# First attention of a two-block network: one v tile ahead of the step loop, projection groups a step earlier, row transposes issued later

The kernel runs on one core of one Trainium2 chip. The metric is the device time of one execution in microseconds. Where a ratio is given, it is the mean time of one kernel's runs over the mean of the kernel before's runs in the same rounds, so it is not quite the ratio of the medians quoted beside it.

## The reference

```python
# x: 2048 rows of 576, four residual layers A, B, A, B on normed rows
def _A_ref(x, wqkv, wo):              # 32 heads of 18, window of 8 positions, every second one
    qkv = (x @ wqkv)...               # q, k, v
    logits = einsum(q, gathered k) * 18 ** -0.5; masked where the position is negative
    return softmax(logits) @ gathered v @ wo
def _B_ref(x, w_in, w_sp, b_sp, w_out):
    z = gelu(x @ w_in)                # 4608 wide, two halves z1, z2
    g = w_sp @ layernorm(z2) + b_sp   # 2048 x 2048 over the rows
    return (z1 * g) @ w_out
x = x + _A_ref(layernorm(x), ...); x = x + _B_ref(layernorm(x), ...)   # twice
```

The change concerns the first A layer alone.

## The kernel before

Attention runs in 38 steps, two for each tile of 112 query rows (16 heads each). A step computes the next step's logits, exponentiates them on ScalarE, multiplies this step's probabilities with v (`PV`), and then runs whatever the table `at(step, ...)` lists for it: projection groups (`PG`) for the second half of the sequence, v tiles (`VW`), the output projection (`WO`), and the normed rows for the next layer (`LN_XN` on POOL, then `LN_T`, a transposing DMA into `xnT`).

```python
def PG(d, qk, cc, dve, queues=(nc.sync, nc.gpsimd)):
    ...                                   # 5 matmuls 128x512, cast into a staging slot
    for dst, src in moves:                # one copy a head: staging slot -> QK
        self.dma(dst, src, eng=queues[dma_rr[0] % len(queues)])
...
if hf == 1:                               # in PV, after the second half of a tile
    if t < NT - 2:
        nc.sync.dma_start_transpose(out=oT[...], in_=o_t[:nq, :])
...
# the table
for k_, (d, qk, cc) in enumerate(pgs):
    at(2 + k_ if li == 0 else (k_ * PG_END) // len(pgs), PG, d, qk, cc, True)
for t in range(nvw, NT):
    for hh in range(2):
        if li == 0 and t == nvw:
            at(hh, VW, t, hh, True)
        else:
            at(2 * t - 2 + hh, VW, t, hh, 2 * t - 2 + hh >= PG_END and hh == 0)
for i in range(NS):
    ...
    at(s - 5, XO, i);  at(s, WO, i, 0);  at(s + 1, WO, i, 1)
    at(s + 1, LN_STATS, i);  at(s + 2, LN_XN, i);  at(s + 2, XST, i)
    if i < NS - 1:
        at(s + 4, LN_T, i)
...
for k_, (d, qk, cc) in enumerate(pre):    # six projection groups ahead of the loop
    if k_ == (2 if li == 0 else 0):
        L_mm(0); EXP(0)
    PG(d, qk, cc, li > 0 or k_ < 4, q2)
for s in range(NST):
    if s + 1 < NST:
        L_mm(s + 1); EXP(s + 1)
    PV(s)
    for f, a in table.pop(s, []):
        f(*a)
```

In the text, "the copies" are the `QK` moves of `PG`, "o transposes" are those in `PV`, and "row transposes" are `LN_T`. All DMA transposes, about half of the copies, and the row loads and stores go through the SyncE queue; the o transposes of the last two tiles are made by TensorE. A block d of the projection is up to 128 columns of q and of k; d=4 is the last. "Late waits" are waits for o transposes near the end of the loop. A cold step or spell is one at half clock. In the profile lines, `L_ps` are the logits, `O_ps` the product of probabilities and v, `pv` a v tile, `pp` a projection group, `pw` the output projection, and `pz` the first product of layer B.

The softmax here doesn't subtract the row's maximum and nothing guards it: scores larger than these inputs give would overflow.

## Time and profile before

| | before |
|---|---|
| median of three runs | 1196.94 us (1193.07 to 1198.15) |
| span of the profiled run | 1193.7 us |
| TensorE busy | 1182.4 us |
| granted clock, mean | 0.996 |

TensorE is the bound; idle gaps and lowered clock are all that an order of instructions can change. The prediction shows the lines for both: two holes of TensorE in the first attention (hole 1 near 46 us, hole 2 near 90 us), each with a spell at half clock behind it.

### The profile page before, as it was taken

What the parts mean: (1) busy time and instruction counts of PE and PEld (TensorE: products, weight loads), DVE (VectorE), ACT (ScalarE), POOL (GpSimd) and SP (SyncE); (2) the same over time, 40 slices, a digit from 0 to 9 for tenths busy, and PEclk for the clock granted to TensorE, in tenths of its full rate; (3) what the DMA queues carried; (4) which work ended last, traced back from release to release, by engine and by line L of the source; (5) the groups of instructions that cost most, each with busy time, mean ns of one, the idle gap of its engine ahead of it and who ended that gap; (6) DMA issues with size and microseconds to landing.
All of it is one profiled execution on the core that took longest, in us unless ns stands there. A gap on an engine that the chain in (4) does not pass through costs nothing.

```text
span 1193.7 us, 20761 instructions
## 1 busy us (share of the span) xinstructions
PE 1182.4 (99%) x8554; PEld 621.8 (52%) x8554; DVE 548.0 (46%) x1207; ACT 376.0 (31%) x592; POOL 275.3 (23%) x383
## 2 busy tenths in 40 slices
PE   9999999999999999999999999999999999999998
PEld 5566644444444444457755775444444444444677
DVE  9687677333233233244455776763223223223311
ACT  6477677211111111201156786770110110111000
POOL 4677773100000000001144777530000000000000
PEclk9899999999999999999999999999999999999999
DMA  8989892000000000049646899900000000000332
GB/s 198 190 160 220 166 221 67 23 1 12 12 12 12 12 1 12 2 139 297 169 97 111 190 236 186 224 11 12 12 12 1 12 12 12 12 1 25 127 105 73
DMA packets 178103, 101.21 MB, mean 85 GB/s; under 512 B 134335, under 2 KB 159359, under 8 KB 178008
## 3 DMA queue, kind: packets, MB, share of 16 engines
q1 hardware_dynamic: 165144, 78.13, 30.9%
q0 software_dynamic: 6512, 16.00, 5.2%
q10 hardware_dynamic: 6352, 5.75, 1.6%
q8 instruction: 67, 1.10, 0.4%
q14 instruction: 28, 0.23, 0.1%
HBM read 42.39 MB, written 16.53 MB: 49 GB/s over the span
## 4 chain that ended last, share of the span: by engine, by line
PE 94%; DMA 2%; SPq 1%; POOL 1%; DVE 1%; issue 0%; ACT 0%; DVEq 0%; POOLq 0%
PE pg L879 42%; PE pz L861 12%; PE po L933 12%; PE pz L783 11%; PE pp L401 4%; PE pw L493 3%; PE pv L378 3%; PE O_ps L456 3%; PE L_ps L436 2%; PE pzs L783 1%; SPq L77 1%; DMA QK<-win2a 1%; POOL QK L77 1%; DMA oT<-o_t 1%; DMA oT<-in_A_x_dram 1%
## 5 line engine op out<-in xcount | busy, mean ns | idle before, releaser
L879 PE MATMUL pg<-Wq,Z 128*128 128x512 bf16 x2304 | 502.8, 379 | 0.0
L879 PEld LDWEIGHTS <-Z 128*128 128x128 bf16 x2304 | 225.5, 98 | 271.7
L883 DVE TENSOR_TENSOR g_tmp<-pg,ln_xn 128x512 f32<-128x512 f32 x144 | 99.5, 691 | 428.9 <-PE pg L879 428.9
L873 ACT ACTIVATE z1T<-pz 128x1024 bf16<-128x1024 f32 x72 | 73.7, 1023 | 513.9 <-PE pz L861 513.7
L77 POOL DMA_DIRECT2D wout<-in_B_w_out_dram x4 | 4.2, 1062 | 604.6 <-PE pg L879 604.6
L445 ACT ACTIVATE P_sb<-L_ps 128x896 bf16<-128x896 f32 (+1 forms) x152 | 126.9, 888 | 46.6 <-PE L_ps L436 46.3
L933 PE MATMUL po<-wout,Z 128*128 128x288 bf16 x1152 | 141.4, 286 | 0.0
L861 PE MATMUL pz<-xnT,w 128*128 128x512 bf16 (+1 forms) x640 | 136.0, 380 | 0.0
L933 PEld LDWEIGHTS <-Z 128*128 128x128 bf16 x1152 | 112.7, 98 | 28.8
L783 PEld LDWEIGHTS <-xnT 128*128 128x128 bf16 (+1 forms) x800 | 66.3, 97 | 80.9 <-issue 23.7
L783 PE MATMUL pz<-win2a,xnT 128*128 128x512 bf16 x384 | 104.8, 380 | 0.0
L884 DVE TENSOR_TENSOR Z<-g_tmp,z1T 128x512 bf16<-128x512 f32 x144 | 99.6, 692 | 10.1 <-DVE g_tmp L883 0.5
L861 PEld LDWEIGHTS <-w 128*128 128x128 bf16 (+1 forms) x640 | 51.1, 97 | 80.0 <-issue 27.1
L401 PE MATMUL pp<-xnT,wqk_sb 128*128 128x512 bf16 x360 | 82.9, 380 | 0.0
L797 ACT ACTIVATE zp<-pz 128x1024 bf16<-128x1024 f32 x64 | 65.5, 1023 | 36.8 <-PE pz L783 34.2
L241 POOL TENSOR_SCALAR ln_xn<-x_new,ln_mv,ln_rstd 128x576 bf16<-128x576 f32 x32 | 73.3, 2290 | 3.0
L943 DVE TENSOR_TENSOR x_new<-po,xo 128x288 f32<-128x288 f32 (+1 forms) x64 | 28.8, 455 | 87.9 <-PE po L933 83.9
L783 PE MATMUL pz<-win2b,xnT 128*128 128x512 bf16 (+1 forms) x256 | 65.8, 380 | 0.0
L799 DVE CUSTOM_DVE_ANT_0 Z<-zp 128x1536 bf16<-128x1536 bf16 x32 | 56.3, 1760 | 16.1 <-ACT zp L797 16.0
L77 POOL DMA_DIRECT2D QK<-stg x81 | 50.7, 631 | 39.0 <-DVE stg L370 23.6
L378 PE MATMUL pv<-wv_sb,xnT 128*128 128x288 bf16 (+1 forms) x380 | 57.6, 291 | 0.0
L401 PEld LDWEIGHTS <-wqk_sb 128*128 128x128 bf16 x360 | 33.3, 98 | 36.1 <-issue 0.5
(112 smaller groups left out, 892.1 us busy)
## 6 DMA issues: line engine op xcount, KB each, us to landing
xres<-x_new SPq DMA_DIRECT2D x48, 288.0 KB
xo<-xres SPq DMA_DIRECT2D x32, 288.0 KB
wout<-in_B_w_out_dram POOLq DMA_DIRECT2D x4, 1296.0 KB, 8.4
xo<-xres SPq DMA_DIRECT2D x8, 576.0 KB
w<-in_B_w_in_dram SPq DMA_DIRECT2D x16, 256.0 KB
QK<-stg POOLq DMA_DIRECT2D x53, 72.0 KB, 4.1
QK<-stg SPq DMA_DIRECT2D x41, 72.0 KB
xo<-in_A_x_dram SPq DMA_DIRECT2D x8, 288.0 KB
```

The lines of the kernel that those rows point to most:

```text
L77: return eng.dma_start(out=out, in_=in_)
L241: e.tensor_scalar(out=xn[:nrows, 0:D], in0=x_t[:nrows, :], scalar1=mv[:nrows, 0:1], scalar2=rstd[:nrows, 0:1], op0=ALU.subtract, op1=ALU.mult)
L378: nc.tensor.matmul(pv[:nk, 0:288], lhsT=self.xnT[:, c, QT * t:QT * t + nk], rhs=wv_sb[:, c, hh * 288:(hh + 1) * 288], start=(c == 0), stop ...
L401: nc.tensor.matmul(pp[:, :], lhsT=w, rhs=self.xnT[:, c, PADL + cc * 512:PADL + (cc + 1) * 512], start=(c == 0), stop=(c == 4))
L445: nc.scalar.activation(out=P_bufs[(2 * s + jp) % 4][:nk, :, :, 0:nq], in_=Lv[:nk, :, :, 0:nq], func=ACT.Exp, scale=scale)
L783: nc.tensor.matmul(pzvs[ci][:, sub * 512:sub * 512 + w], lhsT=self.xnT[r0:r1, c, PADL + i * P:PADL + (i + 1) * P], rhs=win2(c)[r0:r1, c0 + ...
L861: nc.tensor.matmul(pz1s[q // 2][:, q % 2, :], lhsT=w1[r0:r1, c, sub * P:(sub + 1) * P], rhs=self.xnT[r0:r1, c, PADL + q * 512:PADL + (q + ...
L873: nc.scalar.activation(out=z1T[:, q2 * 512:(q2 + 2) * 512], in_=pz1s[q2 // 2][:, :, :].rearrange("p a b -> p (a b)"), func=ACT.Gelu_apprx_ ...
L879: nc.tensor.matmul(pg[:, :], lhsT=Z[:, jj, i, sub * P:(sub + 1) * P], rhs=Wq[q][:, i, :], start=(i == 0), stop=(i == NS - 1))
L883: nc.vector.tensor_tensor(out=tmp[:], in0=pg[:, :], in1=bsp[:, qs], op=ALU.add)
L884: nc.vector.tensor_tensor(out=uT(jj)[:, sub, qs], in0=tmp[:], in1=z1Ts[jj, sub][:, qs], op=ALU.mult)
L933: nc.tensor.matmul(acc[hh], lhsT=uT(j // 2)[:, j % 2, i * P:(i + 1) * P], rhs=wouts[j // NJH][:, j % NJH, hh * 288:(hh + 1) * 288], start= ...
```

## The change

Its intent: fill the first hole with v work, have the copies of the second half issued sooner, and keep the row transposes off the SyncE queue until the copies are through. Meanwhile the normed rows need room. Counted in blocks of 128 rows (`i` in the code), blocks 0 to 3 and 13 to 15 use the four usual buffers, blocks 4 to 12 the three staging slots, which are free by then; the text calls this parking.

```diff
--- before.py
+++ after.py
@@ -227,10 +227,11 @@
                                 op0=ALU.mult, op1=ALU.mult)
         return mv, rstd, nmr
 
-    def ln_xn(self, x_t, nrows, mv, rstd, nmr, eng="act", dup=True):
+    def ln_xn(self, x_t, nrows, mv, rstd, nmr, eng="act", dup=True, xn=None):
         nc = self.nc
-        xn = self.xn_bufs[self.xn_rr % len(self.xn_bufs)]
-        self.xn_rr += 1
+        if xn is None:
+            xn = self.xn_bufs[self.xn_rr % len(self.xn_bufs)]
+            self.xn_rr += 1
         if eng == "act":
             nc.scalar.activation(out=xn[:nrows, 0:D], in_=x_t[:nrows, :], func=ACT.Identity,
                                  scale=rstd[:nrows, 0:1], bias=nmr[:nrows, 0:1])
@@ -503,7 +504,11 @@
 
         def LN_XN(i):
             mv, rstd, nmr = tails[i].pop("ln")
-            tails[i]["xn"] = self.ln_xn(tails[i]["x"], P, mv, rstd, nmr, eng="pool")
+            xn = None
+            if li == 0 and 4 <= i < 4 + 3 * NSTG:
+                k_, m = divmod(i - 4, 3)
+                xn = stgs[(2 + k_) % NSTG][:].rearrange("p a b -> p (a b)")[:, 640 * m:640 * (m + 1)]
+            tails[i]["xn"] = self.ln_xn(tails[i]["x"], P, mv, rstd, nmr, eng="pool", xn=xn)
 
         def LN_T(i):
             self.ln_T(tails.pop(i)["xn"], i * P, P)
@@ -626,7 +631,7 @@
                     R_(12, 4)
                     A_(12, 13, 14, 15)
             T_(12, 13, 14, 15)
-            nvw0, nvw = 4, 8
+            nvw0, nvw = 4, 9
         else:
             for k_, (d, cc) in enumerate([(d, cc) for d in range(5) for cc in range(2)]):
                 for qk in ((1, 0) if d < 4 else (0,)):
@@ -641,7 +646,7 @@
                 if k_ == 6:
                     self.fill_window_rows(QK, 1)
             nvw0, nvw = 0, 4
-        for t in range(nvw0, nvw):
+        for t in range(nvw0, nvw - (1 if li == 0 else 0)):
             for hh in range(2):
                 VW(t, hh, li == 0)
 
@@ -662,11 +667,11 @@
         PG_END = 14
         pre, pgs = pgs[:6], pgs[6:]
         for k_, (d, qk, cc) in enumerate(pgs):
-            at(2 + k_ if li == 0 else (k_ * PG_END) // len(pgs), PG, d, qk, cc, True)
+            at(1 + k_ if li == 0 else (k_ * PG_END) // len(pgs), PG, d, qk, cc, True)
         for t in range(nvw, NT):
             for hh in range(2):
                 if li == 0 and t == nvw:
-                    at(hh, VW, t, hh, True)
+                    at(13 * hh, VW, t, hh, True)
                 else:
                     at(2 * t - 2 + hh, VW, t, hh, 2 * t - 2 + hh >= PG_END and hh == 0)
         for i in range(NS):
@@ -679,7 +684,7 @@
             at(s + 2, LN_XN, i)
             at(s + 2, XST, i)
             if i < NS - 1:
-                at(s + 4, LN_T, i)
+                at(max(s + 4, 24 + (5 * i) // 4) if li == 0 else s + 4, LN_T, i)
         if li == 0:
             at(0, self.load_wo, nc.sync)
             for f in reversed(self.load_win2a(nc.gpsimd)):
@@ -696,6 +701,9 @@
             PG(d, qk, cc, li > 0 or k_ < 4, q2)
             if li == 0 and k_ == 3:
                 self.fill_window_rows(QK, 1)
+        if li == 0:
+            VW(nvw - 1, 0, False)
+            VW(nvw - 1, 1, False)
         for s in range(NST):
             if s + 1 < NST:
                 L_mm(s + 1)
```

Before the loop stood v tiles up to 7, with tile 8 in steps 0 and 1 and tile 9 in 16 and 17. Now tile 8 stands just ahead of the loop, tile 9 is in steps 0 and 13, and the groups of the second half are in steps 1 to 12 instead of 2 to 13.

## The prediction

> **What bounds the kernel now.** I read the page first. TensorE is busy 1182.4 of 1193.7 us and the chain that ended last is 94% TensorE, so only two things can shorten the run: idle gaps of TensorE (11.3 us in all) and stretches in which its clock is lowered. The slices show where those lie:
>
> ```profile
> PE   9999999999999999999999999999999999999998
> PEclk9899999999999999999999999999999999999999
> ```
>
> One slice is 29.8 us. Only the second falls to 8 in the clock, and it covers the start of the first attention. The change touches that stage alone, so next I read its busy time in stretches of 4 us (columns: stretch, length, busy us and instruction count of PE, PEld, DVE, ACT, POOL, then the granted clock, DMA share, GB/s):
>
> ```profile
> 44.00:48.00 4.00, 2.35 (x22) 0.98 (x20) 4.00 (x5) 1.67 (x3) 3.65 (x4) 0.95 1.19 182
> 48.00:52.00 4.00, 3.62 (x58) 2.35 (x59) 2.29 (x6) 2.35 (x4) 2.36 (x4) 0.50 1.06 352
> 52.00:56.00 4.00, 4.00 (x73) 2.20 (x72) 2.00 (x5) 2.73 (x4) 0.00 (x0) 0.69 1.40 286
> ...
> 88.00:92.00 4.00, 2.39 (x43) 1.63 (x42) 2.16 (x8) 2.70 (x5) 3.52 (x4) 1.00 0.35 73
> 92.00:96.00 4.00, 4.00 (x49) 2.53 (x48) 2.31 (x6) 1.69 (x3) 3.80 (x5) 0.57 0.94 249
> ```
>
> Two holes, near 46 and near 90 us, each followed by a spell at half clock. In stretches of 0.5 us the low clock runs from about 47.6 to 54.3 us and from 92.0 to 95.1 us. Elsewhere between 36 and 140 us TensorE is idle only twice, 0.43 us each, for an exponential on ScalarE. The order of TensorE's instructions in time says what the holes are:
>
> ```profile
> 45.37 0.32 PE L436 MATMUL L_ps<-QK 32*128 32x112 bf16 x6
> 46.65 0.20 PE L436 MATMUL L_ps<-QK 32*128 32x112 bf16 x1 [0.96 <-DMA QK<-win2a]
> 47.24 0.46 PE L436 MATMUL L_ps<-QK 32*128 32x112 bf16 x8 [0.39 <-DMA QK<-win2a]
> 48.38 0.27 PE L436 MATMUL L_ps<-QK 32*128 32x112 bf16 x1 [0.68 <-DMA QK<-win2a]
> 48.59 0.60 PE L456 MATMUL O_ps<-v_ext,P_sb 128*128 128x19 bf16 x16
> ...
> 89.01 0.39 PE L436 MATMUL L_ps<-QK 32*128 32x112 bf16 x14
> 90.84 0.22 PE L436 MATMUL L_ps<-QK 32*128 32x112 bf16 x1 [1.45 <-DMA QK<-stg]
> 91.22 0.22 PE L436 MATMUL L_ps<-QK 32*128 32x112 bf16 x1 [0.16 <-DMA QK<-stg]
> ```
>
> Both times the logits wait for the copies that spread q and k rows to their heads: in hole 1 those of the first half of the sequence (2.03 us idle), in hole 2 the last two heads, fed by block d=4 of the second half (1.61 us idle). Why the second copies are late is on the SyncE queue, which issues them in program order:
>
> ```profile
> 81.36 1.24 SPq L248 DMA_TRANSPOSE xnT<-ln_xn  x1
> 82.65 0.57 SPq L77 DMA_DIRECT2D xres<-x_new  x1
> 83.32 1.97 SPq L468 DMA_TRANSPOSE oT<-o_t  x1
> 85.38 3.10 SPq L77 DMA_DIRECT2D QK<-stg  x4
> ```
>
> The cast that makes their data ends at 81.1 us (VectorE: start 80.41, 0.69 long), yet they are issued from 85.38: the queue is full with issuing from about 64 us on.
>
> **What the Trainium skill says.** "TensorE: Matmul & The Clock Gate", section "Part 1: The HAM clock gate", gives two clock states, half and full, set by activity in a free-running window of about 3.4 us. The trace agrees: 0.50 or 1.00, and the low spells are about 6.7 and 3.1 us, two windows and one. "DMA: Bandwidth & Descriptors", section "Issuing engines are not separate DMA queues", says the issuer matters only for sequencer time, usually small beside the transfer; here it isn't small: about 0.8 us a copy and 1.2 to 2.0 a transpose, on a full queue. The same page, "DMA Transpose (X-bar)", keeps plain transposes to SyncE and ScalarE, so the row transposes cannot move to POOL, only in time.
>
> **The change part by part.** No arithmetic is added or removed; the order of instructions has the same count on TensorE. A step is one pass of the attention loop, counted by the start of its O_ps group: step 0 at 48.59, 1 at 50.84, 2 at 53.25, 3 at 55.56, 8 at 66.06, 14 at 81.24, 16 at 85.09, 18 at 91.37, 19 at 94.62 us.
>
> (a) Both halves of v tile 8 move from steps 0 and 1 to just before the first waiting logits. At full clock half a tile is five matmuls taking 0.63 us on the chain, so TensorE is busy until about 46.6 instead of 45.4 us. The copies land when they did (their issue is upstream of everything changed), so step 0 still starts near 48.6, with 1.25 us of work already done and only about 0.8 us idle left. Then the window ending near 47.4 us is nearly all busy and I expect no half clock.
>
> (b) One half of tile 9 goes to step 0, the other to step 13; the projection groups start at step 1 and end at 12. Sum, with pitches read from before:
> - step 0, half a v tile: ScalarE sets it, two exponentials of 0.81 to 0.92 us: 1.9 us (estimate; before took 2.25 cold)
> - steps 1 to 7, projection only: 7 x 2.10 (before, steps 3 to 7: (66.06 - 55.56) / 5) = 14.7
> - steps 8 to 12, projection and output: 5 x 2.53 (before, steps 8 to 13: (81.24 - 66.06) / 6) = 12.65
> - step 13, v and output: 2.2 (before, steps 16 and 17: 2.18 each)
> - steps 14 to 17, output alone: 4 x 1.92 (before, steps 14 and 15: (85.09 - 81.24) / 2), ScalarE again = 7.7
>
> Together 39.15 us, so step 18 starts at 87.7. Before it would have started at 89.45 without its wait (87.27 + 2.18) and did at 91.37. So (a) and (b) give 1.75 us net: about 1.25 for the filled hole and 1.6 for the clock, less about 1.1 because steps 16 and 17 lose fillers and become ScalarE's.
>
> (c) Hole 2. With the groups a step earlier and no row transpose before them (the first moves to step 24), step 12 starts at about 75.3 and block d=4 is cast by 77.7. SyncE issues the d=3 copies at 72.7 to 76.0, then x row store 0.55, one o transpose 1.2 to 2.1, one load 0.44, with gaps 78.4 to 79.3; the four d=4 copies take 3.1 to 3.3, end 81.6 to 82.6; before, the waited matmul started 2.7 us after the last issue, so data at 84.3 to 85.3. Needed near 87.4. Hole 2 closes with 2 us to spare: gain 1.92 (91.37 - 89.45) plus the cold steps after it, 3.25 + 2.25 against 2 x 2.2, 1.1. In all 3.0 us.
>
> (d) Parking rows 4 to 12 in staging slots adds no instruction. It only lets the POOL norm run while transposes wait; the slots' copies are long done at step 18.
>
> (e) Fifteen row transposes now fall into steps 24 to 41, one per 1.25 steps. Per two steps (4.4 us) SyncE issues one o transpose, one or two row transposes, one store, half a load: 3.5 to 4.7 us. Full again: a few transposes of 2 us would delay the last o transposes. The last before came at 127.25, its consumer (pw) started at 130.96, so with issue and landing there is about 1 us of room. I charge 0.4 us.
>
> Sum: 1.75 + 3.0 - 0.4 = 4.35 us. All of it is at the start of one of four layers; what follows is TensorE without gaps and simply starts earlier. From the mean of the three timed runs, 1196.05: 1191.7 us.
>
> **The rivals.**
> 1. The clock falls anyway. Before, the window from about 47.4 to 50.8 us, with 0.68 us idle, did not bring the clock back. If 0.7 us idle also lowers it, or four ScalarE-bound steps in a row (14 to 17, some 0.3 us idle each) do, then 1 to 1.5 us of the gain is lost: 1193. Against it: windows with 0.43 us idle kept the full clock.
> 2. Hole 2 stays because the queue, not the step, decides: SyncE is equally full before the moves. Then only (a) and part of (c) remain, 2 us: 1194. Against it: one transpose of 1.24 us and the o transpose of 1.97 us no longer stand ahead of the four copies, and 2 us of margin.
> 3. The wait moves to the o transposes late in the loop (e): 1 to 3 us stall, perhaps a cold window: 1193 to 1195. For it: the sums of 4.7 against 4.4 us.
> 4. More comes back: ScalarE-bound steps run at the 1.62 us that step 15 took rather than 1.92, 1.2 us more: 1190.
>
> **Range and chances.** The three runs before spread over 5 us, and the free-running window moves the cold spells from run to run, so I take about 3 us either way: 1188.5 to 1194.9. Even both holes in full with their cold spells are under 7 us, 0.6%; 2% would be 24 us, which nothing here holds. A slowdown over 2% would need a stall in every step.
>
> **What would show each step right or wrong.** (a): the clock near 1.00 from 44 to 56 us and v matmuls between the last pp and the waiting logits; wrong if it shows 0.5 again. (b): step 18 starting at 87 to 88.5 us. (c): no wait on the QK copies near 87 us, the last d=4 issue on SyncE over by about 82.6. (e): no wait of pw on a transpose after 105 us. Layer B's first matmuls, now at 133.2 us, should come at about 129. The prediction is wrong if that shift is under 1.5 or over 6.5 us, or if the shift is there but the time does not follow.

## The result

| | before | after |
|---|---|---|
| median, six runs each | 1195.24 us (1193.07 to 1198.15) | 1192.80 us (1189.93 to 1194.85) |
| ratio | 1 | 0.9975 (95%: 0.9956 to 0.9994) |
| span of the profiled run | 1193.7 us | 1190.8 us |
| TensorE busy | 1182.4 us | 1180.2 us |
| granted clock, mean | 0.996 | 0.998 |

The interval lies below 1. The slices of the page after, against those in the prediction:

```profile
PE   8999999999999999999999999999999999999998
PEclk9999999999999999999999999999999999999999
```

The clock row has no 8 any more. (The 8 of the PE row is the first 29.8 us, which end before anything that was changed.) The same stretches of 4 us of the kernel after (stretch, length, busy us and count of PE, PEld, DVE, ACT, POOL; granted clock, DMA share, GB/s):

```profile
44.00:48.00 4.00, 3.92 (x35) 2.17 (x33) 3.93 (x4) 1.97 (x5) 3.43 (x4) 1.00 1.08 176
48.00:52.00 4.00, 3.31 (x61) 2.03 (x59) 3.12 (x7) 3.21 (x4) 3.05 (x5) 0.81 1.09 328
52.00:56.00 4.00, 4.00 (x61) 1.88 (x60) 1.99 (x4) 2.34 (x4) 0.00 (x0) 0.76 1.25 333
...
88.00:92.00 4.00, 4.00 (x84) 3.10 (x79) 3.57 (x12) 3.21 (x4) 3.51 (x5) 1.00 0.96 174
92.00:96.00 4.00, 4.00 (x84) 3.05 (x83) 3.53 (x11) 3.46 (x6) 3.80 (x5) 1.00 1.09 185
```

The second hole is gone with its half clock. The first has shrunk, but a half-clock spell of one window instead of two remains (0.81 and 0.76; in stretches of 0.5 us it runs from about 50.5 to 53.8 us). TensorE in time, after:

```profile
45.96 1.39 PE L379 MATMUL pv<-wv_sb,xnT 128*128 128x288 bf16 x10
47.28 0.89 PE L437 MATMUL L_ps<-QK 32*128 32x112 bf16 x15
48.86 0.22 PE L437 MATMUL L_ps<-QK 32*128 32x112 bf16 x1 [0.69 <-DMA QK<-win2a]
49.01 0.56 PE L457 MATMUL O_ps<-v_ext,P_sb 128*128 128x19 bf16 x16
...
50.90 2.29 PE L402 MATMUL pp<-xnT,wqk_sb 128*128 128x512 bf16 x5
...
125.22 0.79 PE L494 MATMUL pw<-wo_sb,oT 128*128 128x288 bf16 x5 [0.59 <-DMA oT<-o_t]
...
131.51 1.39 PE L494 MATMUL pw<-wo_sb,oT 128*128 128x288 bf16 x10 [1.23 <-DMA oT<-o_t]
```

The ten v matmuls sit in hole 1, where the waits for copies are 0.69 us against 2.03 before. The projection group at 50.90 takes 2.29 us (the next ones 1.24), so it ran at half clock. And 1.82 us of new waits stand near the end of the loop, for o transposes. On SyncE the copies of block d=4 now stand at 80.99 instead of 85.38:

```profile
78.44 0.46 SPq L77 DMA_DIRECT2D xres<-x_new  x1
79.01 1.26 SPq L469 DMA_TRANSPOSE oT<-o_t  x1
80.38 0.52 SPq L77 DMA_DIRECT2D xo<-in_A_x_dram  x1
80.99 3.79 SPq L77 DMA_DIRECT2D QK<-stg  x4
```

To see where time goes in one trace without the noise of the rest, I use anchors: the starts of the probability products (O_ps) of steps 0, 18 and 36, the first matmul of layer B's gating product (pg), and the end. The stretches in us, from the timelines of all runs ("rows" are row transposes):

| trace | step 0 starts | 0 to 18 | 18 to 36 | 36 to gate | gate to end |
|---|---|---|---|---|---|
| before | 48.59 | 42.78 | 40.53 | 82.70 | 979.1 |
| after | 49.01 | 39.30 | 40.02 | 84.07 | 978.4 |
| after again (e1) | 47.70 | 38.88 | 39.13 | 85.49 | 979.0 |
| after again (e8) | 47.91 | 40.36 | 39.35 | 84.68 | 980.2 |
| v tiles only (e2) | 48.90 | 40.14 | 44.84 | 82.72 | 978.4 |
| rows only (e3) | 46.80 | 40.90 | 39.16 | 85.24 | 978.9 |
| rows from 18 (e4) | 49.35 | 39.40 | 39.12 | 82.73 | 978.4 |
| rows from 18 (e12) | 46.77 | 40.19 | 42.23 | 82.71 | 978.4 |
| rows from 28 (e5) | 48.56 | 38.33 | 39.13 | 90.08 | 978.4 |
| two tiles ahead (e6) | 48.80 | 41.32 | 39.17 | 85.51 | 978.4 |
| two tiles, rows from 18 (e7) | 48.62 | 40.26 | 40.25 | 82.67 | 979.7 |
| loads spread (e9) | 49.09 | 42.04 | 39.13 | 84.94 | 979.1 |
| rows 18, loads spread (e10) | 46.98 | 40.16 | 40.06 | 82.90 | 978.5 |
| before, loads spread (e11) | 47.57 | 45.34 | 41.50 | 82.69 | 978.7 |

Step 0 itself starts up to 2.6 us sooner or later from trace to trace, and the last stretch takes 978.4 to 980.2 us, a spread that was not followed up. The gain after is 3.48 us in steps 0 to 18 and 0.51 us up to step 36; 1.37 us is given back between step 36 and the gate, where the 1.23 us wait lies. That column splits by where the row transposes start: 82.67 to 82.90 us in the seven traces that start them as before or from step 18, 84.07 to 85.51 us in the six from step 24, and 90.08 us from step 28.

### The profile page after: what moved, and what is told of

Read it like the earlier page. It is cut to its first block, busy times and chain, and to the rows that moved or that the text cites. A ratio compares the mean times of both kernels' runs of the same rounds, so it can differ in the third digit from the quotient of the medians.

```text
span 1190.8 us, 20761 instructions
## 1 busy us (share of the span) xinstructions
PE 1180.2 (99%) x8554; PEld 620.6 (52%) x8554; DVE 547.4 (46%) x1206; ACT 376.6 (32%) x593; POOL 281.5 (24%) x383
## 4 chain that ended last, share of the span: by engine, by line
PE 94%; DMA 3%; POOL 1%; ACT 0%; issue 0%; SPq 0%; DVE 0%; ACTq 0%; DVEq 0%
PE pg L887 42%; PE pz L869 12%; PE po L941 12%; PE pz L791 11%; PE pp L402 5%; PE pw L494 3%; PE O_ps L457 3%; PE pv L379 3%; PE L_ps L437 2%; DMA oT<-o_t 2%; PE pzs L791 1%; DMA QK<-win2a 1%; POOL QK L77 1%; DMA wqk_sb<-in_A_wqkv_dram 1%; ACT P_sb L446 0%
## 5 line engine op out<-in xcount | busy, mean ns | idle before, releaser
L791 PE MATMUL pz<-win2a,xnT 128*128 128x512 bf16 x384 | 104.8, 380 | 0.0
L242 POOL TENSOR_SCALAR ln_xn<-x_new,ln_mv,ln_rstd 128x576 bf16<-128x576 f32 x23 | 52.8, 2294 | 2.0
```

Of the source, the lines that this page charges most:

```text
L791: nc.tensor.matmul(pzvs[ci][:, sub * 512:sub * 512 + w], lhsT=self.xnT[r0:r1, c, PADL + i * P:PADL + (i + 1) * P], rhs=win2(c)[r0:r1, c0 + ...
```

## The experiments

Twelve kernels ran, in four groups; each group shares a chip and its own eleven runs of the kernel before. All gave correct results. The effects are a few tenths of a per cent, so I read each mechanism in the trace and use the ratios for the sum.

**e1 and e8: the changed kernel again**, unaltered, as a yardstick of its group.

> The changed kernel unaltered, as the yardstick of this group. Theory (both parts are needed: the v tiles fill hole 1, the later row transposes close hole 2): ratio to before 0.997 to 0.998, step 18 near 88.3 us, no wait on the copies of block d=4, 1 to 2 us of waiting of pw for o transposes after 120 us. Noise rival (the 2.4 us between the medians are run-to-run scatter): ratio 0.999 to 1.001.

Measured: 1191.78 us, ratio 0.9979 (0.9963 to 0.9995).

> The changed kernel once more, as the yardstick of this group: ratio to before about 0.998, waits of pw for o transposes of 1 to 2 us between 120 and 132 us.

Measured: 1192.23 us, ratio 0.9981 (0.9965 to 0.9998). With the first result three groups give 0.9975, 0.9979 and 0.9981, each interval below 1: the gain is real, and the three estimates are 2.3 to 3.0 us (0.19% to 0.25% of 1195), each with an interval of some 2 us either way. The late waits for o transposes in the first attention were 1.25 us in e1 and 2.04 us (0.15 and 1.89) in e8. e1 kept the full clock through the whole of 44 to 56 us; e8 fell to half in the same place as the first trace (0.84 and 0.73 in the two stretches). In e1 the late wait itself was followed by half clock (0.69 and 0.89 in the stretches from 128 to 136 us), which the first trace and e8 did not show; the waiting group took 2.02 us there and 1.39 us in the first trace:

```profile
128.91 2.02 PE L494 MATMUL pw<-wo_sb,oT 128*128 128x288 bf16 x10 [1.25 <-DMA oT<-o_t]
```

So between step 36 and the gate e1 took 2.79 us more than the trace before, not 1.25.

**e2: only the v tiles and groups move.**

```diff
-            if li == 0 and 4 <= i < 4 + 3 * NSTG:
+            if False:
...
-                at(max(s + 4, 24 + (5 * i) // 4) if li == 0 else s + 4, LN_T, i)
+                at(s + 4, LN_T, i)
```

> Only the v tiles and projection groups are moved; row transposes where they were. Theory: hole 1 filled as in the changed kernel; on SyncE one row transpose (1.25 us) stands again ahead of the d=4 copies, which then are issued until about 86 us and land near 88.7, against 87.8 wanted: a wait of 0 to 1.2 us at step 18, without a cold spell; no wait for o transposes late. Time 1192 to 1194. Rival (the delay of the row transposes does nothing for hole 2, the earlier projection groups do it alone): no wait at all at step 18, no late wait either, so 1190.5 to 1192, faster than the changed kernel.

Measured: 1194.47 us, ratio 1.0008 (0.9987 to 1.0029). Neither theory holds as a whole. There is no wait on the copies of the second half at all, as the rival had it; but the time is that of the kernel before. Hole 1 kept 1.07 us of waits and its half clock (0.65 and 0.93 from 48 to 56 us). TensorE's waits between 60 and 140 us (engine, line, what for: total, times, longest), first before, then this kernel, then the changed kernel:

```profile
PE L_ps L436 <- DMA QK<-stg: 1.6, 2, 1.5
PE L_ps L436 <- ACT P_sb L445: 0.9, 2, 0.4
```

```profile
PE pw L494 <- DMA oT<-o_t: 4.7, 3, 2.9
PE L_ps L437 <- ACT P_sb L446: 0.9, 3, 0.3
```

```profile
PE pw L494 <- DMA oT<-o_t: 1.8, 2, 1.2
PE L_ps L437 <- ACT P_sb L446: 0.9, 3, 0.3
```

The wait for the copies has turned into a larger one for o transposes, at 85.8, 91.4 and 109.4 us. SyncE of e2 shows how:

```profile
85.17 1.23 SPq L249 DMA_TRANSPOSE xnT<-ln_xn  x1
86.44 0.58 SPq L77 DMA_DIRECT2D xres<-x_new  x1
87.13 2.42 SPq L469 DMA_TRANSPOSE oT<-o_t  x1
...
101.03 1.23 SPq L249 DMA_TRANSPOSE xnT<-ln_xn  x1
102.35 0.53 SPq L77 DMA_DIRECT2D xres<-x_new  x1
102.93 0.42 SPq L77 DMA_DIRECT2D xo<-in_A_x_dram  x1
103.46 1.94 SPq L469 DMA_TRANSPOSE oT<-o_t  x1
```

Once the groups run a step sooner, the first row transpose already stands behind the d=4 copies (they are listed first in the same step), so delaying it buys the copies nothing. But each pair of steps takes the queue about 4 us, nearly as long as TensorE needs for it, and it was still behind at 103 us: the o transpose issued at 103.46 had its data at about 98.3 (VectorE's product for that tile ended then), and the matmul that wants it starts at 109.38. That is 5.2 us of queue and 4 us from the end of issue to the start of the matmul. The wait at 85.8 lies before this queue can be blamed: its o transpose was issued at 79.80, ahead of every row transpose.

**e3: only the row transposes move**, with parking; v tiles and groups as before.

```diff
-            nvw0, nvw = 4, 9
+            nvw0, nvw = 4, 8
...
-            at(1 + k_ if li == 0 else ..., PG, ...)
+            at(2 + k_ if li == 0 else ..., PG, ...)
...
-                    at(13 * hh, VW, t, hh, True)
+                    at(hh, VW, t, hh, True)
...
-        if li == 0:
-            VW(nvw - 1, 0, False)
-            VW(nvw - 1, 1, False)
```

> Only the row transposes are later (with parking); v tiles and projection groups as before. Theory: hole 1 and its cold spell stay as before (2.0 us idle, half clock to about 54 us); the d=4 copies are issued 1.25 us sooner than in the kernel before, so the wait at step 18 shrinks from 1.6 to about 0.4 us and its cold spell goes; the late wait of 1 to 2 us for o transposes appears. Together 1194 to 1196, within noise of before. Rival (the row transposes had nothing to do with hole 2): the wait at step 18 stays at 1.4 to 1.7 us and the late wait is added: 1196 to 1198.

Measured: 1193.43 us, ratio 0.9998 (0.9981 to 1.0015). The wait in hole 2 is 1.01 us against 1.61 before, not the 0.4 us that the theory named, and its cold spell is gone. A late wait of 1.02 us appears, which this trace puts down to VectorE's `o_t` and not to a transpose, with half clock behind it (0.75 and 0.83 from 128 to 136 us); the two take 2.5 us back between step 36 and the gate. Its hole 1 was only 0.51 us in this trace, without a cold spell, although the code up to there is that of the kernel before: hole 1 is a matter of when copies land, and it varies.

So the parts measure 1.0008 and 0.9998 alone and 0.9975 to 0.9981 together. The intervals of the parts reach down to 0.9987 and 0.9981, so a small gain of one alone is not ruled out. The earlier groups, for which the move of the v tiles makes room, close hole 2: none of the eleven traces that have them waits for those copies. With them alone the wait goes to the o transposes in the middle of the loop (4.7 us in e2); with the row transposes later as well these waits were absent there (after, e1, e8), and smaller ones came late.

**e4 and e12: row transposes from step 18** instead of 24.

```diff
-                at(max(s + 4, 24 + (5 * i) // 4) if li == 0 else s + 4, LN_T, i)
+                at(max(s + 4, 18 + (5 * i) // 4) if li == 0 else s + 4, LN_T, i)
```

> The changed kernel, but the row transposes start at step 18 instead of 24, still after the d=4 copies. Theory (the late waits come from SyncE issuing 15 row transposes in too few steps): hole 2 stays closed, the waits of pw for o transposes after 120 us (1.8 us in the changed kernel) fall to 0 to 0.4 us, time 1 to 2 us below the changed kernel. Rival (the late waits come from the transfers, not the queue, or from the earlier steps): they stay at 1 to 2 us.

Measured: 1191.06 us, ratio 0.9979 (0.9961 to 0.9997), beside 1191.78 us and 0.9979 of e1 in the same group. Its trace has no wait for an o transpose in the whole first attention, as the theory said, though hole 1 had 1.52 us of waits and half clock (0.76 and 0.81 from 48 to 56 us); the times do not tell it from the changed kernel.

> The version with row transposes from step 18 again, on whatever chip this falls: is it better than the changed kernel, whose three ratios were 0.9975 to 0.9981? If the absence of late waits seen once is the rule, 0.996 to 0.9975 and no wait of pw above 0.5 us after 120 us; if waits only move with the landing of o transposes, 0.998 again with a wait of about 1 us somewhere between steps 10 and 38.

Measured: 1190.03 us, ratio 0.9955 (0.9931 to 0.9979), the lowest of all, but with a wait of 1.71 us for an o transpose at 104.8 us, where e2 had its longest, and 1.36 us for a row transpose of the first norm. So in these traces the row transposes' start decides where the wait may fall, not whether there is one: the loss between step 36 and the gate is gone in all four traces from step 18 (e4, e7, e10, e12), but three of them wait elsewhere. The ratios of this version, 0.9979 and 0.9955, lie within and below the range of the changed kernel (0.9975 to 0.9981); that it is better is not shown, since the one group that held both has them equal.

**e5: row transposes from step 28**, one a step.

```diff
-                at(max(s + 4, 24 + (5 * i) // 4) if li == 0 else s + 4, LN_T, i)
+                at(max(s + 4, 28 + i) if li == 0 else s + 4, LN_T, i)
```

> A larger dose of the suspected cost: row transposes start at step 28 and come one a step. Theory (row transposes crowd the o transposes off the SyncE queue late in the loop): the waits of pw for o transposes grow from 1.7 to 3 us or more, time 1 to 2 us above the changed kernel. Rival (the late waits have another cause, such as the norm on POOL or the faster steps themselves): they stay at 1 to 2 us and the time is that of the changed kernel.

Measured: 1196.61 us, ratio 1.0011 (0.9996 to 1.0026), 3.6 us above the changed kernel by the ratios (0.9981 to 1.0011 of 1195). The time went up, but the theory's place was wrong: the waits for o transposes fell to 0.8 us. TensorE lost it in layer B. Waits of e5 between 130 and 150 us, whole lines of that view:

```profile
POOL ln_xn L77 <- DMA xnT<-ln_xn: 9.3, 1, 9.3
DVE Z L807 <- DMA xnT<-ln_xn: 8.4, 1, 8.4
ACT Z L809 <- DMA xnT<-ln_xn: 5.5, 1, 5.5
...
PE pz L791 <- ACT zp L805: 3.9, 1, 3.9
```

The first sums of squares of layer B write into memory that attention used, and in the built program those two instructions wait on nearly all DMA semaphores (the trace has eight semaphore instructions ahead of one and nine ahead of the other, the last at 142.4 us), so on the last row transposes as well. The one that the trace names reads a usual buffer (`ln_xn`), not a slot. ScalarE stands in order behind its own (5.5 us), cannot empty PSUM, and TensorE waits 3.9 us and then runs at half clock (0.50 in the stretch 144 to 148 us). In the table this is the 90.08 against 84 to 85.5. In the changed kernel the same instruction of VectorE waits for its input (2.7 us), not for transfers. So the row transposes have a last date, which step 24 meets and step 28 does not.

**e6: both tiles 8 and 9 ahead of the loop**, groups from step 0.

```diff
-            nvw0, nvw = 4, 9
+            nvw0, nvw = 4, 10
...
-            at(1 + k_ if li == 0 else ..., PG, ...)
+            at(k_ if li == 0 else ..., PG, ...)
...
-            VW(nvw - 1, 0, False)
-            VW(nvw - 1, 1, False)
+            for t in (8, 9):
+                VW(t, 0, False)
+                VW(t, 1, False)
```

> Both tiles 8 and 9 (four groups of five matmuls, 2.5 us) go before the waiting logits, and the projection groups run at steps 0 to 11. Theory (idle time in hole 1 is what lowers the clock, and filling it whole keeps it up): idle in hole 1 0 to 0.4 us in place of 0.2 to 0.7, no half clock between 44 and 58 us, step 18 38.2 to 38.8 us after step 0; but the late waits for o transposes stay at 1.5 to 2.5 us. Time 0 to 1 us below the changed kernel. Rival (the clock falls from the small matmuls and the ScalarE-bound steps, not from the hole): a spell at half clock in the same stretch all the same.

Measured: 1194.96 us, ratio 0.9988 (0.9970 to 1.0006). Hole 1 has no idle left, as the theory said, and yet the clock falls (0.89 and 0.68 in the stretches from 48 to 56 us), because a new hole opens behind it:

```profile
48.47 0.39 PE L437 MATMUL L_ps<-QK 32*128 32x112 bf16 x16
48.80 0.56 PE L457 MATMUL O_ps<-v_ext,P_sb 128*128 128x19 bf16 x16
51.43 0.59 PE L402 MATMUL pp<-xnT,wqk_sb 128*128 128x512 bf16 x1 [2.07 <-DMA xnT<-ln_xn]
```

The first group of the second half reads rows whose transposes (of the first norm) were issued from 42.20 to 47.40 us and had not all landed. In the changed kernel that group is a step later; even there it waited 0.47 (e1) and 0.43 us (e8). The late wait was 1.48 us, as expected. So in this trace the groups came too soon for their rows; whether they always would is not shown (see e7).

**e7: the same with row transposes from step 18** (the edits of e6 and e4 together).

> The former with the row transposes from step 18, the candidate for the best. Theory: hole 1 filled, hole 2 closed, no late waits beyond 0.5 us: 1 to 2 us below the changed kernel, ratio to before about 0.996 to 0.997. Rival (faster steps 12 to 17 only bring the o transposes into the way at steps 14 to 20): waits of pw of 1 to 3 us there and the time of the changed kernel.

Measured: 1193.14 us, ratio 0.9984 (0.9969 to 0.9999). The rival: waits of pw for o transposes of 1.88 us at 85.3 and 0.86 us at 91.1, with a half-clock spell (0.77 and 0.80 from 84 to 92 us). In this trace the group did not wait for its rows, and 44 to 56 us ran at full clock.

**e9, e10, e11: the weight loads of layer B spread** over steps 2 to 7 in the changed kernel (e9), in the version from step 18 (e10) and in the kernel before (e11).

```diff
-            for f in reversed(self.load_win2a(nc.gpsimd)):
-                at(0, f)
+            for n_, f in enumerate(reversed(self.load_win2a(nc.gpsimd))):
+                at(2 + n_, f)
```

> The changed kernel, but the six weight loads of layer B that POOL issues in one go at about 46 to 51 us come one a step at steps 2 to 7. Theory (hole 1 and the wait of the first projection group are late landings, because those 1.7 MB fill the transfer engines just then): the copies land up to 1 us sooner, idle in hole 1 plus the wait of pp for the row transposes 0 to 0.3 us in place of 0.4 to 0.7, no half clock between 47 and 55 us; late waits for o transposes unchanged at 1.5 to 2 us. Ratio to before 0.996 to 0.9975. Rival (the copies are late because they are issued late, by data and queue): hole 1 and the clock as in the changed kernel, ratio 0.998.

> The same with the row transposes from step 18: the candidate for the best. Theory: hole 1 nearly empty and no late wait: all of the first attention without a TensorE wait above 0.5 us except for ScalarE, ratio to before 0.995 to 0.9965. Rival (waits only move: the loads now collide with the copies of the second half or the first o transposes): new waits of 1 us or more at steps 3 to 18, ratio 0.998.

> The kernel before with only the loads spread. Theory: idle in hole 1 falls from 2.0 to about 1 to 1.5 us (the logits still come before the copies can land) and its cold spell is rarer; hole 2 stays at 1 to 2 us: ratio 0.9985 to 0.9995. Rival (issue, not transfer): hole 1 unchanged, ratio 1.000.

Measured: e9 1196.74 us, ratio 1.0001 (0.9974 to 1.0027); e10 1193.94 us, 0.9985 (0.9963 to 1.0006); e11 1197.25 us, 1.0015 (0.9989 to 1.0041). None gains. Waits for copies in hole 1 were 0.98 us in e9, none in e10 and 0.76 us in e11, and none of the three fell to half clock between 44 and 56 us, nor did any wait for the rows of the first norm. But five of the eleven traces without the edit kept the full clock there too, so three traces do not show that spreading did it. What came instead: 2.03 us (e9) and 0.80 us (e10) of waiting for o transposes near 71 to 74 us, and in e11 2.52 us at hole 2 and three pauses (1.24, 0.87 and 0.69 us) for which the trace names no releaser. The rival of e10 holds in the main: waits moved, though its new ones were 0.80, 0.63 and 0.32 us, smaller than it said; e9 also kept a late wait of 0.93 us with half clock behind it (0.63 from 132 to 136 us).

## Why the prediction was right, and where its sizes were off

The three results are 1191.8, 1192.2 and 1192.8 us, with 1191.7 predicted. The drop, 2.3 to 3.0 us by the ratios, is smaller than the 4.35 us of the sum; that the number came out nearly right is in part luck, because the later medians of the kernel before lie mostly below the 1196.05 that I started from (1195.24, and 1193.64 to 1196.52 in the four groups). The prediction's own tests: layer B's first matmuls came at 129.67 us against 133.24, a shift of 3.6 us, and the time followed by 2.9 us in that trace; step 18 started at 88.31, inside 87 to 88.5 (86.58 in e1, 88.27 in e8); "no half clock" and "no wait of pw after 105 us" failed.

**(a) Hole 1: half right.** The filler went where the prediction put it, and the waits for copies were 0.69, 0.24 and 0 us in the three traces (about 0.8 predicted). But the same start left 1.07, 1.52, 0.87 and 0 us in e2, e4, e5 and e12, and the unchanged start left 2.03 us before and 0.51 us in e3, so how much of this the filler did is not shown. "No half clock" held in one trace of three, and in three of those seven. In the first, the step with the slow group took 3.18 us (50.46 to 53.64) against 2.10 for its like: 1.1 us, rival 1's estimate of 1 to 1.5. In e8 the wait for the first norm's rows did its part, which the prediction did not have at all.

**(b) The steps: near, by two errors that cancel.** 39.15 us from step 0 to step 18 was the sum; 39.30, 38.88 and 40.36 were measured. At full clock and without a wait for transfers the same steps took 38.33 us (e5): steps 1 to 13 fit the sum, but step 0 took 1.45 us against 1.9 and steps 14 to 17 took 7.36 (80.95 to 88.31 after) against 7.7. In the first trace the cold step that the sum left out, 1.1 us, filled the difference; in e8 a cold step and a wait more than filled it.

**(c) Hole 2: right in outcome, partly wrong in reason.** No trace with the groups a step earlier waits for those copies. In the first trace their issue ended at 84.78, later than the 81.6 to 82.6 of the estimate (the d=3 copies alone took 4.58 us), in e1 at 82.96; the margin was thinner than the 2 us given. And e2 shows that, with the groups earlier, hole 2 closes without the delay of the row transposes. Rival 2 falls. "Only in time" was too narrow: the section that the prediction cites names ScalarE beside SyncE as an issuer of transposes; moving the row transposes there was not tried.

**(d) Parking "adds no instruction": true, but the delay that it allows is not free.** Layer B's first instructions wait for the last row transposes, and e5 shows the price of issuing these too late: 3.9 us of TensorE and a cold spell.

**(e) The late waits: the term that was mis-sized.** I charged 0.4 us; waits of 1.82, 1.25 and 2.04 us were measured, and with the cold spell of e1 the loss between step 36 and the gate was 1.37, 2.79 and 1.98 us against the trace before. Rival 3 named this at 1 to 3 us, "perhaps a cold window". The estimate paired the wrong instructions: by the order of the program the last o transpose (127.25 before) feeds the output group at 133.68, not that at 130.96, so there was more room before, about 5 us; and the change uses it up. After, the same two stand at 126.80 and 131.51: the transpose came 0.45 us sooner, its consumer was wanted some 3.4 us sooner (131.51 less 1.23 of waiting), and it started 3.5 us after the issue had ended, which I had taken as much shorter. What the term should have said, as these times show: TensorE gains, SyncE does not, so the difference comes out of the o transposes' slack.

**The clock as part of the gain.** In the 44 runs of the kernel before that have a clock, 23 have a mean of 0.997 or less (mean time 1196.3 us) and 19 of 0.999 or more (1193.6 us). Of 17 runs of the changed kernel, 2 are low and 14 high (1191.8 us). Among high-clock runs of the pool the change is worth 1.8 us of 2.7, and the low means became rare; but in the two experiment groups that hold both kernels (e1, e8) the high-clock runs differ by 1.8 and 2.8 us, so the clock's share of the gain is not settled. The groups ran on different chips, so this is a count and not a comparison of the same rounds. The spell that went is that of hole 2 (0.57 before; full clock there in all three traces of the changed kernel), not that of hole 1. The one profile that I predicted from, at 0.996, was one of the worse cases, so part of the 4.35 us was probably there only in about half of the runs.

**Still open.** What made the wait at 85.8 us in e2, and why o transposes take about 4 us to land in some traces, was not separated into queue and transfer. What the filler in hole 1 is worth would need more traces of both starts. Whether starting at step 18 beats step 24 would need both in more common rounds.

## What to carry to other kernels

When a step loop runs faster, every queue that feeds it in program order loses slack: add up its issue times per step and see who stands behind whom, for after the change, not before. A part that shows no gain alone (here 1.0008 and 0.9998) can be needed by the other part, so test both alone and together. And read more than one trace: where a hole depends on landing times and on a clock window, one profile can show much more than the next (2.03 and 0.51 us here, for the same code).

## What the Trainium skill lacked or had wrong

- "TensorE: Matmul & The Clock Gate", "Part 1: The HAM clock gate": the two states (0.50 and 1.00) and the window hold here, with low spells of about 6.7 and 3.1 us before and 3.3 us after. Its table ties the low state to an idle window of about 3.4 us; further down it also names short idles between groups, and nowhere does it give a share of idle time that suffices. Here partly idle stretches sufficed: 1.61 us of waiting before, and 0.69 us after, while 0.16 and 0.71 us in e5 kept the full clock in the same place. The threshold is not settled by these runs.
- "DMA: Bandwidth & Descriptors", "Issuing engines are not separate DMA queues": it calls the sequencer's time usually small beside the transfer. Here four copies took SyncE 3.1 to 4.9 us and an o transpose 1.2 to 3.2 us to issue, and the queue's order decided which transfer was late (5.2 us between data ready and issue in e2).
- The same page, "DMA Transpose (X-bar)": no time from issue to landing of a transpose within SBUF under load. Here matmuls that waited for one started 3.5 us (after) and 4.0 us (e2) after the end of its issue.
- No page that I used has a cost for the first write into memory taken over from an earlier stage whose transfers are still open; e5 shows waits of 8.4 us on VectorE and 5.5 us on ScalarE.
